# A float64-weight attention and gated feed-forward kernel on one core: conversions begun inside the first attention pass and done in halves, the second queries loaded ahead of the values, and the first value means written in place

## The chip, the cores and the metric

The kernel runs on one NeuronCore of a Trainium2 chip. The metric is device time of one execution in microseconds (us). A core has a matrix engine (PE, with weight loads shown as PEld), a vector engine (DVE), a scalar engine (ACT), a GpSimd engine (POOL) and a queue that issues DMA transfers (SP). Each engine runs its own instructions strictly in their order and waits on semaphores for the others.

## The reference

```python
scores_l = scale * q @ k.T                     # |i - j| < 16 kept, else -1e9
k_sum    = max of k over blocks of 32 keys     # 24 per head
v_sum    = mean of v over blocks of 32 keys
scores_s = scale * q @ k_sum.T + log(32)
a        = softmax(concat(scores_l, scores_s)) # denominator + 1e-9
attn     = a @ concat(v, v_sum)                # (4, 8, 768, 64)
x        = attn as (3072, 512)
out      = (x @ w_a * (x @ w_b)) @ w_out       # d_ff = 1536
```

q, k and v are float32. The three weight matrices are float64 in memory: `w_a` and `w_b` are 512 x 1536, `w_out` is 1536 x 512.

## The kernel before, in words

The 3072 tokens are cut into 12 units of 256 tokens (u = 0 to 11), three to each of four batches. A unit has an attention pass, `attention(u)`, over two tiles of 64+64 queries, and then 12 items (u, f), one for each slice of 128 of the 1536 hidden columns. An item is `hidden(u, f)`: 24 matmuls of 128x256 into one PSUM bank (12 with w_a, 12 with w_b), then `g` on ACT and DVE (L586, L587), then its split into `gh` (ACT, L590) and `gl` (POOL, L591). `down(u, f)` adds its 6 matmuls of 128x512 into `po` (L569).

Each float64 weight is turned on the chip into two float32r tiles, `hi` and `lo`. There are 36 conversions: slices f = 0 to 11 of w_a, w_b and w_out, called a0, b0, o0, a1 and so on. One conversion (`convert_weights`) is one ACT instruction (L159, `p`), four DVE instructions of 128x512 in a chain (L161 into PSUM tile `s`, L164 into `f`, L170 into `s`, L173 into `p`), an ACT copy to `hi` (L181) and two POOL instructions (L182, L183, the second gives `lo`). `raw` and `w` have the same memory, so L181 overwrites what L173 has read. The tiles `f` and `p` come from the pool `stage` (six buffers, tag t2k). A raw load waits for the conversion four before it (`AHEAD = 4`).

The head of the program is written out by hand: `load_first` loads k, q and v of unit 0; `attention(0)` runs to its end; then nine conversions are written; then the items, the first `LAG = 5` of them of unit 0 alone, and after them unit 1 and unit 0 by turns. Each of the first items brings three conversions with it, later ones two. A scheduler then orders each engine's instructions by a time model of its own, so that the program order is a priority rather than an order; the order that comes out is fixed when the kernel is built. The k loads of batch 1 (`blocks`, L293) wait for the last conversion.

In the head, `sum_first_v` makes the 24 block means of v with six matmuls of 24x512, copies them to a tile `vs` (L208), and `load_vsums` (L402) moves `vs` by four DMAs into the rows of the value tiles `vw` that `av` (L480) reads. Two of the six v tiles lie in `pt` and one in `kin` and one in a `stage` buffer; the second tile's scores `s1` and its two value tiles take four more `stage` buffers, so that five of the six buffers are taken by the first attention pass.

Of the kernel before, what the change touches and what calls it, by code (L numbers as in the profile page):

```python
# [21 lines left out]
def attention_moe(  # L22
# [88 lines left out]
    mean = const.tile([P, 2 * NS - 4], F32, name="mean")  # L111
    nc.gpsimd.memset(mean, 0.0)
    for i in range(P // BLK):
        nc.gpsimd.memset(mean[i * BLK : (i + 1) * BLK, NS - 4 + i, None], 1.0 / BLK)
# [27 lines left out]

    def convert_weights():
        for f, nm in ((f, nm) for f in range(NF) for nm in "abo"):
# [3 lines left out]
            low, high = words[:, :, :, 0], words[:, :, :, 1]  # L148
# [5 lines left out]
            fv = fv.rearrange("p (m n) -> p m n", n=n)  # L154
            pv = pv.rearrange("p (m n) -> p m n", n=n)
            sv = ps_a.tile([P, CV], F32, tag="psc", name=f"s_{nm}{f}")
            sv = sv.rearrange("p (m n) -> p m n", n=n)
            fi, pi, si = fv.bitcast(I32), pv.bitcast(I32), sv.bitcast(I32)
            nc.scalar.mul(out=pv, in_=high.bitcast(F32), mul=2.0**-112)  # L159
# [4 lines left out]
            nc.vector.scalar_tensor_tensor(  # L164
                out=fi, in0=pi, scalar=-(1 << 31), in1=si,
                op0=ALU.bitwise_and, op1=ALU.bitwise_or,
# [3 lines left out]
            nc.vector.tensor_scalar(  # L170
                out=si, in0=fi, scalar1=-(1 << 23), scalar2=None, op0=ALU.bitwise_and
            )
            rest = nc.vector.scalar_tensor_tensor(  # L173
                out=pv, in0=low.bitcast(U32), scalar=2.0**-52, in1=sv,
                op0=ALU.mult, op1=ALU.mult,
            )
# [22 lines left out]
    def sum_first_v():  # L199

        ps = psum("vs0", 0)
        for i in range(S // P):
            nc.tensor.matmul(  # L203
                ps[:NS], mean[:, NS - 4 - 4 * i : 2 * NS - 4 - 4 * i], first["v"][i],
                start=(i == 0), stop=(i == S // P - 1),
            )
        vsums[0] = att.tile([NS, H, D], F32, tag="vs", name="vs0", bufs=1)
        nc.scalar.copy(out=vsums[0].rearrange("p h d -> p (h d)"), in_=ps[:NS])  # L208
# [35 lines left out]

    def load_first():

        shape = [P, 2, 512]
        spots = [  # L250
            xp.tile(shape, F32, tag="x0", name="k_in0"),
            xp.tile(shape, F32, tag="x1", name="k_in1"),
            att.tile(shape, F32, tag="qin", name="k_in2", bufs=1),
        ]
        first["k"] = [t[:, i, :] for t in spots for i in range(2)]
        t = xp.tile(shape, F32, tag="x0", name="q_in0")
        first["q"] = t
        t = xp.tile(shape, F32, tag="x1", name="v_in0")
        first["v"] = [t[:, i, :] for i in range(2)]
        first["v"].append(kin[:, :512])  # L260
        first["v"].append(stage.tile([P, 512], F32, tag="t2k", name="v_in3"))
        first["v"] += [pbuf[:, i].rearrange("p c x -> p (c x)") for i in range(2)]
        for nm, i in (
            [("k", i) for i in range(6)] + [("q", 0)] + [("v", i) for i in range(6)] + [("q", 1)]
        ):
            xin = first[nm][:, i, :] if nm == "q" else first[nm][i]
            src = {"k": k, "q": q, "v": v}[nm]
# [4 lines left out]
            yield  # L272

# [105 lines left out]
    def load_v(b, t, spare=False):  # L379

        if spare:
            vw = [stage.tile([P, H, D], F32, tag="t2k", name=f"vw{b}_{t}_{e}") for e in range(2)]
            nc.gpsimd.memset(vw[0][WIN:], 0.0)
            nc.gpsimd.memset(vw[1][32:64], 0.0)
        else:
            vw = vbuf
# [103 lines left out]
    def attention(u):  # L490
# [10 lines left out]
        if u == 0:  # L501
            s1 = [
                stage.tile([P, 512], F32, tag="t2k", name=f"s1_{h}").rearrange(
                    "p (c x) -> p c x", x=P
                )
                for h in range(2)
            ]
        vw = load_v(b, t0)
        qT = prep_q(u, 0, qin)
        yield  # L510
        scores(u, t0, qT, s)
        yield
        qT = prep_q(u, 1, qin)
        yield
        if u == 0:
            scores(u, t1, qT, s1)
            yield
        if r == 0:
            if u == 0:
                sum_first_v()  # L520
            else:
                for hg in range(2):
                    sum_v(b, hg)
                    yield
            load_vsums(b, vw)
        if u == 0:
            vw1 = load_v(b, t1, True)
            load_vsums(b, vw1)
        transp(u, t0, s)
        yield  # L530
        if u:
            scores(u, t1, qT, s1)
# [3 lines left out]
        if u:  # L536
            vw1 = load_v(b, t1)
# [59 lines left out]
    LAG = 5  # L597
# [81 lines left out]
```

## Time and profile before

| | us |
|---|---|
| median of 3 runs | 759.15 (758.52 to 760.43) |
| the profiled execution | 756.2 |
| its span, first to last instruction | 754.3 |

| engine | busy us | share of the span |
|---|---|---|
| PE | 718.0 | 95% |
| PEld | 644.0 | 85% |
| DVE | 410.6 | 54% |
| ACT | 275.9 | 37% |
| POOL | 254.2 | 34% |

A row of a timeline gives the start, the duration (for several merged instructions from the first's start to the last's end), engine, line, operation, output and inputs, shapes, a count, and in brackets the idle time of the engine before it with what ended it. [...] A row of the table by stretches gives the stretch, its length, busy time of PE, PEld, DVE, ACT and POOL with instruction counts, the granted share of the PE clock, the mean busy share of the DMA engines and GB/s moved.

### The profile page before, as it was taken

The numbers are of one execution on the slowest core, as the hardware profiler recorded it, in microseconds if no ns is written. First come the engines' busy times: TensorE is split into PE (matmuls) and PEld (weight loads), VectorE is DVE, ScalarE is ACT, GpSimd is POOL, SyncE is SP. The second block draws the span as 40 slices with busy tenths as digits, with TensorE's granted clock in tenths as the row PEclk, the third lists the DMA queues.
The fourth block names the chain that finished last, engine by engine and source line by source line (L and its number), as shares of the span: only waits on it lengthen the run. The fifth ranks groups of instructions, "written<-read, shape, count | busy, mean of one in ns | idle before, by whom it ended". The sixth has DMA issues, their size and how long they took to land.

```text
span 754.3 us, 15201 instructions
## 1 busy us (share of the span) xinstructions
PE 718.0 (95%) x5964; PEld 644.0 (85%) x5964; DVE 410.6 (54%) x870; ACT 275.9 (37%) x856; POOL 254.2 (34%) x333
## 2 busy tenths in 40 slices
PE   6778899989999999999999999999999999999997
PEld 3467788879899999998999999998999899999996
DVE  3599999965555444366565444367465444344100
ACT  3678765533232322313233422313233423322212
POOL 4467889962122212212122212213122312212111
PEclk9879899999999999999999999999999999999999
DMA  9956546446502103035302103024302101000000
GB/s 220 209 148 181 166 141 185 143 65 114 148 7 50 50 8 64 29 50 101 119 8 50 51 7 65 30 44 90 112 9 50 50 2 44 29 1 21 29 1 29
DMA packets 155888, 55.05 MB, mean 73 GB/s; under 512 B 136376, under 2 KB 148664, under 8 KB 155816
## 3 DMA queue, kind: packets, MB, share of 16 engines
q1 hardware_dynamic: 155816, 54.07, 29.8%
q8 instruction: 47, 0.77, 0.4%
q14 instruction: 25, 0.20, 0.1%
HBM read 47.12 MB, written 6.29 MB: 71 GB/s over the span
## 4 chain that ended last, share of the span: by engine, by line
PE 70%; DVE 14%; POOL 5%; DMA 5%; issue 2%; SPq 2%; ACT 1%; ACTq 0%; DVEq 0%; POOLq 0%
PE h L552 40%; PE po L569 22%; PE s L423 4%; PE av L480 2%; DMA kin<-in_k_dram 2%; SPq L293 1%; DVE pt L472 1%; PE vs L203 1%; DVE s_b L161 1%; POOL f_b L182 1%; POOL w_b L183 1%; DVE kT L325 1%; DVE f_a L164 1%; DVE vp L221 1%; DVE p_a L173 1%
## 5 line engine op out<-in xcount | busy, mean ns | idle before, releaser
L552 PEld LDWEIGHTS h<-x,w_a 128*128 128x128 f32 x1728 | 231.0, 191 | 25.6 <-DVE g L587 8.5
L552 PE MATMUL h<-x,w_a 128*128 128x256 f32 x1728 | 242.1, 283 | 6.8 <-DVE g L587 6.7
L552 PE MATMUL h<-x,w_b 128*128 128x256 f32 x1728 | 225.4, 278 | 2.2 <-POOL w_b L183 2.2
L591 POOL TENSOR_TENSOR gl<-g,gh 128x256 fp32r<-128x256 f32 x144 | 105.8, 737 | 341.8 <-ACT gh L590 324.8
L552 PEld LDWEIGHTS h<-x,w_b 128*128 128x128 f32 x1728 | 211.3, 189 | 4.3 <-POOL w_b L183 2.4
L569 PE MATMUL po<-w_o,gh 128*128 128x512 f32 x576 | 172.4, 404 | 6.2 <-ACT gh L590 6.1
L587 DVE TENSOR_TENSOR g<-h,g 128x256 f32<-128x256 f32 x144 | 59.5, 418 | 192.0 <-ACT g L586 191.4
L586 ACT COPY g<-h 128x256 f32<-128x256 f32 x144 | 52.4, 370 | 227.7 <-PE h L552 225.9
L569 PEld LDWEIGHTS po<-w_o,gh 128*128 128x128 f32 x576 | 98.1, 189 | 25.0 <-ACT gh L590 7.5
L590 ACT CAST gh<-g 128x256 fp32r<-128x256 f32 x144 | 58.0, 406 | 143.5 <-DVE g L587 143.4
L569 PE MATMUL po<-w_o,gl 128*128 128x512 f32 x288 | 100.8, 398 | 0.1
L472 DVE STREAM_TRANSPOSE pt<-s 32x256 f32<-32x256 f32 x216 | 94.3, 436 | 11.4 <-POOL s L452 8.4
L441 ACT ACTIVATE s<-s,nml 128x128 f32<-128x128 f32 x192 | 74.6, 390 | 40.4 <-DVE nml L436 40.4
L452 POOL TENSOR_TENSOR s<-s,nml 128x512 f32<-128x512 f32 x40 | 41.6, 1041 | 98.7 <-DVE nml L447 93.5
L569 PEld LDWEIGHTS po<-w_o,gl 128*128 128x128 f32 x288 | 51.1, 190 | 9.2 <-POOL gl L591 1.0
L430 DVE SCALAR_TENSOR_TENSOR s<-s,mask 128x512 f32<-128x512 f32 x48 | 31.8, 683 | 25.2 <-PE s L423 23.2
L423 PE MATMUL s<-kT,qT 64*64 64x128 f32 x768 | 43.2, 286 | 1.0 <-POOL kT L348 0.8
L423 PEld LDWEIGHTS s<-kT,qT 64*64 64x64 f32 x768 | 31.0, 137 | 9.0 <-issue 1.4
L480 PE MATMUL av<-pt,vw 128*64 128x64 f32 x768 | 31.5, 231 | 5.2 <-DMA vw<-vs 3.8
L446 DVE TENSOR_SCALAR nml<-nml 128x4 f32<-128x4 f32 x48 | 10.7, 223 | 46.9 <-ACT s L441 46.9
L441 ACT ACTIVATION_READ_ACCUMULATOR s<-s,nml 128x1 f32 x192 | 36.0, 187 | 0.0
L480 PEld LDWEIGHTS av<-pt,vw 128*64 128x64 f32 x768 | 26.8, 142 | 10.4 <-ACT s L441 4.0
(81 smaller groups left out, 493.2 us busy)
## 6 DMA issues: line engine op xcount, KB each, us to landing
raw_a<-in_moe_w_a_dram SPq DMA_DIRECT2D x12, 512.0 KB
raw_b<-in_moe_w_b_dram SPq DMA_DIRECT2D x12, 512.0 KB
raw_o<-in_moe_w_out_dram SPq DMA_DIRECT2D x12, 512.0 KB
out_dram<-ob SPq DMA_DIRECT2D x24, 256.0 KB
qin<-in_q_dram SPq DMA_DIRECT2D x144, 32.0 KB
vb<-in_v_dram SPq DMA_DIRECT2D x24, 192.0 KB
kin<-in_k_dram SPq DMA_DIRECT2D x46, 100.0 KB
vw<-in_v_dram SPq DMA_DIRECT2D x20, 192.0 KB
```

The costliest lines, as they stand in the source:

```text
L423: nc.tensor.matmul(banks[h][es, c, :], qT[hs, c, es], kT[hs, c, c0 : c0 + P], start=True, stop=True, tile_position=(h * D, e * QT),)
L430: nc.vector.scalar_tensor_tensor(out=s[h], in0=banks[h], scalar=0.125, in1=mask[:, kind, None, :].broadcast_to([P, NP, P]), op0=ALU.mult, ...
L441: nc.scalar.activation(s[h][:, c, :], s[h][:, c, :], AF.Exp, bias=nml[:, 0, h, c : c + 1], scale=1.0, accum_out=nml[:, 1, h, c : c + 1],)
L452: nc.gpsimd.tensor_tensor(out=s[h], in0=s[h], in1=l[:, :, None].broadcast_to([P, NP, P]), op=ALU.mult)
L472: nc.vector.transpose(out=pv[js, :, qs], in_=sv[qs, :, js])
L480: nc.tensor.matmul(ps[h * D : (h + 1) * D, c, es], vw[e][:, 2 * c + h, :], pbuf[:, h, c, es], start=True, stop=True, tile_position=(0, h * D),
L552: nc.tensor.matmul(ps, wts[nm, f][:, c, part, :], x[xpart][:, c, :], start=(i == 0), stop=(i == n - 1))
L569: nc.tensor.matmul(po[j], g[:, js], w[:, 0, part, :], start=(f == 0 and i == 0), stop=(f == NF - 1 and i == 2),)
L586: nc.scalar.copy(out=g, in_=pa)
L587: nc.vector.tensor_tensor(out=g, in0=pb, in1=g, op=ALU.mult)
L590: nc.scalar.copy(out=gh, in_=g)
L591: nc.gpsimd.tensor_tensor(out=gl, in0=g, in1=gh.bitcast(F32), op=ALU.subtract)
```

## The change

Five edits, all in the first fifth of the program.

1. A conversion's four DVE instructions of 512 columns become eight of 256 columns, two halves by turns, through one PSUM tile `scratch` that all conversions share.
2. Two conversions (a0, b0) are written behind the first scores, one (o0) behind the second scores, and six at the end of `attention(0)`, where nine stood. `LAG` is 4 instead of 5.
3. The second queries are loaded ahead of the weights and of v, and the v loads take pairs of rows (runs of 512 bytes instead of 256).
4. k, q, v, `s1` and the second value tiles of the first pass lie in nine tiles (`spot`) that later hold the weights of f = 11, 10 and 9, so that they take no `stage` buffer, no `kin` and no `pt`.
5. The block means of v are made by twelve matmuls of 128x256 with a wide indicator matrix `mean` (one memset, two small memsets, four selects on POOL), whose output has the 24 means and 8 zero rows already on the rows that `vw` needs. Four ACT copies (L234) write them there. The four DMAs are gone, and so are two memsets.

```diff
-    mean = const.tile([P, 2 * NS - 4], F32, name="mean")
+    mean = const.tile([P, P + 16], F32, name="mean")
...
+    scratch = ps_a.tile([P, CV], F32, tag="psc", name="scratch")
...
+            parts = []
+            for i in range(2):
+                cols = slice(i * CV // 2, (i + 1) * CV // 2)
+                parts.append((fv[:, cols], pv[:, cols], scratch[:, cols], lows[:, cols]))
+            for fx, px, sx, _ in parts:
+                nc.vector.tensor_scalar(
+                    out=sx.bitcast(I32), in0=px.bitcast(I32), scalar1=3, scalar2=None,
+                    op0=ALU.logical_shift_left,
+                )
...
-            nc.vector.tensor_scalar(
-                out=si, in0=pi, scalar1=3, scalar2=None, op0=ALU.logical_shift_left
-            )
...
-        for i in range(S // P):
-            nc.tensor.matmul(
-                ps[:NS], mean[:, NS - 4 - 4 * i : 2 * NS - 4 - 4 * i], first["v"][i],
-                start=(i == 0), stop=(i == S // P - 1),
-            )
-        vsums[0] = att.tile([NS, H, D], F32, tag="vs", name="vs0", bufs=1)
-        nc.scalar.copy(out=vsums[0].rearrange("p h d -> p (h d)"), in_=ps[:NS])
+        for g in range(2):
+            for i in range(3):
+                for j in range(2):
+                    nc.tensor.matmul(
+                        ps[:, g * 256 : (g + 1) * 256], mean[:, 16 - 8 * i : 16 - 8 * i + P],
+                        first["v"][3 * g + i][:, :, j * D : (j + 1) * D],
+                        start=(i == j == 0), stop=(i == 2 and j == 1),
+                    )
+        for vw in vws:
+            for e, r0 in ((0, WIN), (1, 32)):
+                rows = slice(r0, r0 + 32)
+                nc.scalar.copy(out=vw[e][rows].rearrange("p h d -> p (h d)"), in_=ps[rows])
...
-            [("k", i) for i in range(6)] + [("q", 0)] + [("v", i) for i in range(6)] + [("q", 1)]
...
+        for nm, i in [("k", i) for i in range(6)] + [("q", 0), ("q", 1)]:
...
+    def spot(i):
+
+        return wp.tile([P, 2, 512], F32, tag=f"w{'abo'[i % 3]}{NF - 1 - i // 3}", name=f"spot{i}")
...
-    LAG = 5
+    LAG = 4
...
-    take(rest, 7)
+    take(rest, 8)
     take(weights, 2)
-    take(rest, 7)
-    for _ in attention(0):
-        pass
+    take(rest, 6)
+    first_attention = attention(0)
+    take(first_attention, 8)
+    take_weights(2)
+    take(first_attention, 2)
+    take_weights(1)
+    take(first_attention, 100)
+    take_weights(6)
     atts = {u: attention(u) for u in range(1, NU)}
-    take_weights(9)
```

The order on DVE behind the last maximum of k (`ks`), before. `s` and `s1` are the scores of the two tiles of unit 0, `nml` their maxima and sums.

```order
L315 TENSOR_REDUCE ks0_208<-tr_k5_249 128x4x4
L430 SCALAR_TENSOR_TENSOR s_171<-s0_0_0_275,mask_94 128x512
L430 SCALAR_TENSOR_TENSOR s_171<-s0_0_1_278,mask_94 128x512
L436 TENSOR_REDUCE nml0_0_293<-s_171 128x4 x2
...
L430 SCALAR_TENSOR_TENSOR s1_1_264<-s0_1_1_322,mask_94 128x512
L436 TENSOR_REDUCE nml0_1_337<-s1_0_263 128x4
L161 TENSOR_SCALAR s_a0_442<-p_a0_441 128x512
L436 TENSOR_REDUCE nml0_1_337<-s1_1_264 128x4
L164 SCALAR_TENSOR_TENSOR f_a0_440<-p_a0_441,s_a0_442 128x512
```

And in the changed kernel, at the same place (`spot7` is the second tile's scores):

```order
L342 TENSOR_REDUCE ks0_212<-tr_k5_253 128x4x4
L174 TENSOR_SCALAR scratch_186<-p_a0_322 128x256 x2
L179 SCALAR_TENSOR_TENSOR f_a0_321<-p_a0_322,scratch_186 128x256 x2
L186 TENSOR_SCALAR scratch_186<-f_a0_321 128x256 x2
L191 SCALAR_TENSOR_TENSOR p_a0_322<-raw_a0_202,scratch_186 128x256 x2
L174 TENSOR_SCALAR scratch_186<-p_b0_339 128x256
L456 SCALAR_TENSOR_TENSOR s_171<-s0_0_0_282,mask_94 128x512
L174 TENSOR_SCALAR scratch_186<-p_b0_339 128x256
L456 SCALAR_TENSOR_TENSOR s_171<-s0_0_1_285,mask_94 128x512
L462 TENSOR_REDUCE nml0_0_300<-s_171 128x4
L179 SCALAR_TENSOR_TENSOR f_b0_338<-p_b0_339,scratch_186 128x256 x2
```

All of conversion a0 now stands ahead of the first scores on DVE, and b0 is woven into them; before, a0 began behind the second tile's scores.

The order on ACT in the changed kernel from the first exponentials to the first `av` (`vw0`, `vw1` and `spot8` are the value tiles):

```order
L467 ACTIVATE s_171,nml0_0_300<-s_171,nml0_0_300 128x128 x8
L467 ACTIVATE spot7_267,nml0_1_378<-spot7_267,nml0_1_378 128x128 x4
L163 ACTIVATE p_o0_400<-raw_o0_319 128x512
L467 ACTIVATE spot7_267,nml0_1_378<-spot7_267,nml0_1_378 128x128 x4
L201 CAST w_b0_349<-f_b0_338 128x4x128
L163 ACTIVATE p_a1_496<-raw_a1_336 128x512
L234 COPY vw0_173<-vs0_426 32x512
L234 COPY vw1_174<-vs0_426 32x512
L234 COPY spot8_271<-vs0_426 32x512 x2
L488 COPY pt_172<-pt0_0_0_414 128x512
L201 CAST w_o0_410<-f_o0_399 128x512
L488 COPY pt_172<-pt0_0_1_420 128x512
```

Before, L208 and the first copy to `pt` stood behind the first eight exponentials, and the second tile's exponentials behind both. Now all sixteen, three conversion steps and the four copies stand ahead of `pt`.

The order on DVE behind the last conversion (o11), before (`kT` is built from the k of batch 1, `g1_7` is item (1, 7)):

```order
L173 SCALAR_TENSOR_TENSOR p_o11_1478<-raw_o11_1413,s_o11_1479 128x512
L325 STREAM_TRANSPOSE kT_87<-kin_177 128x6x96
L326 STREAM_TRANSPOSE kT_87<-kin_177 128x6x32
L327 STREAM_TRANSPOSE kT_87<-kin_177 128x32
...
L587 TENSOR_TENSOR g0_11_1818<-h0_11_1793,g0_11_1818 128x256
L587 TENSOR_TENSOR g1_7_1856<-h1_7_1831,g1_7_1856 128x256
```

And now:

```order
L191 SCALAR_TENSOR_TENSOR p_o11_1625<-raw_o11_1554,scratch_186 128x256 x2
L608 TENSOR_TENSOR g0_11_1968<-h0_11_1943,g0_11_1968 128x256
L608 TENSOR_TENSOR g1_8_2006<-h1_8_1981,g1_8_2006 128x256
L512 TENSOR_TENSOR x2_1_2017<-av2_4_2221,x2_0_2016 128x4x128
L352 STREAM_TRANSPOSE kT_87<-kin_177 128x6x96
```

The two products `g` stood behind the transposes of `kT` and now stand ahead of them; beside the last item of unit 0 stands item (1, 8) of unit 1, where it was (1, 7).

## Rows read from the trace of the kernel before

**Rows 1.** The page: the span, and busy tenths of PE and DVE in 40 slices of 18.9 us.

```profile
span 754.3 us, 15201 instructions
...
PE   6778899989999999999999999999999999999997
...
DVE  3599999965555444366565444367465444344100
```

**Rows 2.** Busy time by stretches: start and end, length, then PE, PEld, DVE, ACT, POOL with counts, granted PE clock, DMA share, GB/s.

```profile
15.00:42.50 27.50, 21.72 (x193) 13.11 (x190) 16.86 (x33) 15.43 (x48) 10.29 (x10) 0.88 0.96 205
42.50:112.80 70.30, 58.83 (x473) 50.75 (x472) 65.86 (x116) 54.57 (x160) 53.29 (x46) 0.88 0.54 158
112.80:158.00 45.20, 40.60 (x288) 37.13 (x288) 41.78 (x67) 23.65 (x47) 42.73 (x39) 1.00 0.44 137
158.00:170.00 12.00, 10.13 (x62) 9.44 (x61) 5.93 (x18) 2.49 (x6) 5.11 (x6) 0.86 0.63 101
170.00:754.30 584.30, 577.03 (x4899) 526.89 (x4897) 275.99 (x633) 174.03 (x581) 133.52 (x177) 1.00 0.21 47
```

**Rows 3.** The chain that ended last, from the first scores to the first `av`: start, us, what.

```profile
15.17 1.30 DVE s L430 x2
16.52 7.86 PE vs L203 x12
24.40 0.57 ACT vs L208
25.00 6.01 DMA vw<-vs
...
31.14 1.55 PE av L480 x32
```

**Rows 4.** DVE in order of time, 15 to 42.5 us.

```profile
15.17 1.29 DVE L430 SCALAR_TENSOR_TENSOR s<-s,mask 128x512 f32<-128x512 f32 x2 [2.68 <-PE s L423]
...
26.83 1.29 DVE L430 SCALAR_TENSOR_TENSOR s<-s,mask 128x512 f32<-128x512 f32 x2 [6.14 <-PE s L423]
28.04 0.68 DVE L436 TENSOR_REDUCE nml<-s 128x4 f32<-128x512 f32 x1
28.63 0.68 DVE L161 TENSOR_SCALAR s_a<-p_a 128x512 int32<-128x512 int32 x1
29.22 0.68 DVE L436 TENSOR_REDUCE nml<-s 128x4 f32<-128x512 f32 x1
...
39.42 0.68 DVE L486 TENSOR_TENSOR x<-av,x 128x512 fp32r<-128x512 f32 x1
...
41.81 0.68 DVE L173 SCALAR_TENSOR_TENSOR p_o<-raw_o,s_o 128x512 f32<-128x512 uint32 x1
```

**Rows 5.** DVE in order of time where a conversion follows a conversion, 119 to 125 us.

```profile
119.61 0.69 DVE L161 TENSOR_SCALAR s_a<-p_a 128x512 int32<-128x512 int32 x1
120.41 0.69 DVE L164 SCALAR_TENSOR_TENSOR f_a<-p_a,s_a 128x512 int32<-128x512 int32 x1
121.13 0.69 DVE L170 TENSOR_SCALAR s_a<-f_a 128x512 int32<-128x512 int32 x1
121.86 0.69 DVE L173 SCALAR_TENSOR_TENSOR p_a<-raw_a,s_a 128x512 f32<-128x512 uint32 x1
122.65 0.69 DVE L161 TENSOR_SCALAR s_b<-p_b 128x512 int32<-128x512 int32 x1
...
124.81 0.75 DVE L587 TENSOR_TENSOR g<-h,g 128x256 f32<-128x256 f32 x2
```

**Rows 6.** POOL in order of time, one round of three conversions, 123 to 133 us.

```profile
123.33 1.29 POOL L182 TENSOR_TENSOR f_a<-f_a,w_a 128x512 f32<-128x512 f32 x1 [0.34 <-ACT w_a L181]
124.70 1.28 POOL L183 TENSOR_TENSOR w_a<-f_a,p_a 128x512 fp32r<-128x512 f32 x1
125.93 1.44 POOL L591 TENSOR_TENSOR gl<-g,gh 128x256 fp32r<-128x256 f32 x2
...
132.96 1.29 POOL L182 TENSOR_TENSOR f_a<-f_a,w_a 128x512 f32<-128x512 f32 x1 [0.34 <-ACT w_a L181]
```

**Rows 7.** The chain that ended last, two pieces from 170 us on, where PE alone sets the time: the matmuls of one `hidden` and of one `down`.

```profile
174.92 1.37 PE po L569 x6
176.29 2.75 PE h L552 x24
```

**Rows 8.** DVE in order of time behind the last conversion, 157 to 165 us, and PE beside it.

```profile
157.35 0.69 DVE L173 SCALAR_TENSOR_TENSOR p_o<-raw_o,s_o 128x512 f32<-128x512 uint32 x1
162.29 0.78 DVE L325 STREAM_TRANSPOSE kT<-kin 128x576 f32<-128x576 f32 x1 [4.25 <-DMA kin<-in_k_dram]
...
164.31 0.74 DVE L587 TENSOR_TENSOR g<-h,g 128x256 f32<-128x256 f32 x2
...
164.77 2.78 PE L552 MATMUL h<-x,w_a 128*128 128x256 f32 x12 [1.87 <-DVE g L587]
```

**Rows 9.** Two stretches with the rate of the transfers as the last column: 11 to 13 us (rows of 1 KB, weights) and 14 to 20 us (rows of 256 bytes, v).

```profile
11.00:13.00 2.00, 1.20 (x5) 0.72 (x4) 1.05 (x2) 1.23 (x3) 0.36 (x2) 1.00 1.09 349
14.00:20.00 6.00, 4.55 (x26) 1.39 (x21) 2.82 (x6) 2.91 (x15) 0.70 (x1) 1.00 1.34 218
```

**Rows 10.** The page's costliest groups: the exponentials (mean ns of one behind the comma).

```profile
L441 ACT ACTIVATE s<-s,nml 128x128 f32<-128x128 f32 x192 | 74.6, 390 | 40.4 <-DVE nml L436 40.4
```

**Rows 11.** POOL in order of time, the copy of the key maxima into `kT`.

```profile
12.64 1.05 POOL L348 COPY kT<-ks 128x144 f32<-128x144 f32 x4 [2.76 <-DVE ks L315]
```

More of the change, by code (lines that the diff above doesn't have):

```diff
@@ L243, in turned, with pairs @@
         return tr
+    def pairs(x, b, i, heads=slice(0, H)):
+        return x[b, heads, 256 * i : 256 * (i + 1), :].rearrange("h (p t) d -> p h (t d)", t=2)
     def load_first():
[L249 to L253, printed above, removed]
-        ]
[L255 to L263, printed above, removed]
-            [("k", i) for i in range(6)] + [("q", 0)] + [("v", i) for i in range(6)] + [("q", 1)]
-        ):
+        spots = [spot(i) for i in range(7)]
+        first["k"] = [t[:, i, :] for t in spots[:3] for i in range(2)]
+        first["q"] = spots[3]
+        first["v"] = [
+            t[:, i, :].rearrange("p (h x) -> p h x", x=2 * D) for t in spots[4:] for i in range(2)
+        ]
+        for nm, i in [("k", i) for i in range(6)] + [("q", 0), ("q", 1)]:
             xin = first[nm][:, i, :] if nm == "q" else first[nm][i]
-            src = {"k": k, "q": q, "v": v}[nm]
+            src = k if nm == "k" else q
             nc.sync.dma_start(
@@ L272, in load_first @@
             yield
+        for i, t in enumerate(first["v"]):
+            nc.sync.dma_start(
+                out=t, in_=pairs(v, 0, i % 3, slice(i // 3 * 4, i // 3 * 4 + 4))
+            )
+            yield
+    def spot(i):
+        return wp.tile([P, 2, 512], F32, tag=f"w{'abo'[i % 3]}{NF - 1 - i // 3}", name=f"spot{i}")
     first = {}
@@ L381, in load_v @@
         if spare:
-            vw = [stage.tile([P, H, D], F32, tag="t2k", name=f"vw{b}_{t}_{e}") for e in range(2)]
-            nc.gpsimd.memset(vw[0][WIN:], 0.0)
-            nc.gpsimd.memset(vw[1][32:64], 0.0)
+            spare = spot(8)
+            vw = [spare[:, e, :].rearrange("p (h d) -> p h d", d=D) for e in range(2)]
         else:
@@ L501, in attention @@
         if u == 0:
[L502 to L509, printed above, removed]
+            t = spot(7)
+            s1 = [t[:, h, :].rearrange("p (c x) -> p c x", x=P) for h in range(2)]
+        vw = vw1 = load_v(b, t0)
+        if u == 0:
+            vw1 = load_v(b, t1, True)
+        qTs = [prep_q(u, 0, qin)]
         yield
-        scores(u, t0, qT, s)
+        scores(u, t0, qTs[0], s)
         yield
-        qT = prep_q(u, 1, qin)
+        qTs.append(prep_q(u, 1, qin))
         yield
         if u == 0:
-            scores(u, t1, qT, s1)
+            scores(u, t1, qTs[1], s1)
             yield
[L518 to L524, printed above, removed]
+        if r == 0 and u:
+            for hg in range(2):
+                sum_v(b, hg)
+                yield
             load_vsums(b, vw)
-        if u == 0:
-            vw1 = load_v(b, t1, True)
-            load_vsums(b, vw1)
         transp(u, t0, s)
         yield
+        if u == 0:
+            sum_first_v((vw, vw1))
+            yield
         if u:
-            scores(u, t1, qT, s1)
+            scores(u, t1, qTs[1], s1)
             yield
```

50 lines of the change are left out of this document (30 added, 20 removed).

## The prediction, written before the result was known

> **What bounds the kernel now.** I read the slices of the page first, because a share over the whole span hides stages: PE's digit stays at 9 only from the tenth slice (170 us) on, while DVE's is 9 from the third to the eighth (38 to 151 us) [rows 1]. The table by stretches says the same in numbers. [...] So the tail is work of PE that this change leaves alone; what can be won is what PE stands or runs slowly ahead of 170 us. In 42.5 to 158 that is 70.3 - 58.8 + 45.2 - 40.6 = 16.1 us of standing and about 0.12 x 58.8 = 7.1 us of low clock: 23.2 us.
>
> What holds PE there are the 36 conversions. The three done by 42.5 us end at 41.81 + 0.68 [rows 4], the last at 157.35 + 0.69 [rows 8], so 33 follow in 115.5 us, 3.5 us each. Where nothing stands between them a round of three takes 132.96 - 123.33 = 9.63 us [rows 6]; PE needs 2 x (2.75 + 1.37) = 8.24 us for the two items of a round [rows 7].
>
> **The conversions begin earlier (edits 2, 3, 4).** Between 15 and 42.5 us DVE is busy 16.9 of 27.5 us; the longest gap, 6.14 us, ends with the second tile's scores [rows 2, 4]. Now a0 goes ahead of the first scores and b0 and o0 between the scores, and five `stage` buffers are free for them. Weights a0 come after one more q load of 256 KB, 1.2 us at 218 GB/s [rows 9]. In the trace they are among the 1-KB rows moved from 11 us on, done by about 12 and later now by that 1.2, so DVE can begin near 15 us, when the first scores began. Three conversions earlier, at the 2.9 us that one costs DVE in the filled stretch (below), is 8.6 us. Bounds: nothing, if the inputs come late, and 10 us, all the idle time of the stretch. I take 7, since o0's first step stands on ACT between exponentials and its load now follows six v loads and six value loads, so that both may wait for it.
>
> The price: the first scores' evacuation waits for a0, about 2.7 us. The chain to the first `av` ran from the means (16.52 to 24.38) over a copy of 0.57 and DMAs of 6.01 us to 31.14 [rows 3]. The DMAs go; four copies of about 0.57 come, 2.3 us. That alone would give 6.0 - 1.7 = 4.3 us. But ACT now does all sixteen exponentials, 16 x 0.39 = 6.2 us [rows 10], three conversion steps and the copies ahead of `pt`, so I put unit 0's last `x`, at 39.42 + 0.68 before [rows 4], within 2 us of where it was, at 39 to 42, and count nothing. The wide matmuls stream the same 3,072 columns as before: nothing. On POOL two memsets and four small selects come ahead of the copy into `kT`, where POOL stood 2.76 us waiting for DVE [rows 11], and two memsets go: nothing; without that cover, 1 us.
>
> **The halves (edit 1).** In a dense conversion the steps start 0.80, 0.72, 0.73 and 0.79 us apart, 3.04 together, although one takes 0.69: each waits for the one before [rows 5]. Where independent instructions alternate, 512 columns start 0.59 apart (28.04, 28.63, 29.22) and overlap by some 0.09 [rows 4]. Two `g` of 256 columns end 0.75 after the first began [rows 5]; with the tail of one, 0.42, they start 0.33 apart. Eight halves, each depending on the one two before, are then 8 x 0.33 = 2.64: 0.40 less than the dense chain. In the first 19 conversions other instructions already stand between the steps: the 40 others in that stretch, at their spacing (0.6 for 512 columns, 0.33 for `g`, 0.2 for the small ones), are about 15.5 us, which leaves (70.3 - 15.5)/19 = 2.9 us for a conversion, so the halves give about 0.23 there, 4.4 us. In the last 14 POOL is in the way: of its 9.63 us it stands 0.34 [rows 6], so a round cannot fall below 9.29: 14/3 x 0.34 = 1.6 us. Sum 6.0. Bounds: 33 x 0.40 = 13.2 if POOL never held it, and 13 us lost if halves do not overlap at all (second rival).
>
> **LAG 4 and the end of the conversions (edit 2).** One more item of unit 1 is done by the last conversion, so one less, 2.75 + 1.37 = 4.1 us, stands behind it, if PE keeps up. Also DVE no longer meets the `kT` transposes ahead of the two `g`: before, they waited 4.25 us for a k load and PE 1.87 us for `g` [rows 8]. That 1.87 goes; the k load still comes only after the last conversion and holds the next `g`, by when PE has a hidden item of 2.75 us to do.
>
> **The sum.** From the conversions: 7 + 6 + 4.1 = 17.1 us. PE cannot take all of that. Between 112.8 and 158, at full clock, it still stood 4.6 of 45.2 us, a tenth, because each round has it wait for `g` and for DVE's queue. With the same tenth over the some 102 us that would be left, it loses 10 us; 23.2 - 10 = 13.2 is the most this stretch can give back. I take the smaller, 13.2, add 1.9 for the `kT` stall, and take off 1 for the later first scores: 14 us. The span becomes 754.3 - 14 = 740.3, the profiled execution 742.2 with the 1.9 us around the span. The median of the runs before is 759.15, 2.95 above the profiled execution; on that scale the prediction is 745.1, so 745. With 17.1 + 1.9 and no deduction it is 740; with the conversions' terms halved, 752. The likeliest case's own range is 740 to 751.
>
> **Rivals.**
>
> *All of it passes.* PE hardly waits once unit 1's `x` is there early, its clock stays at the upper level from 40 us on, and DVE fills every gap: 10 + 8 + 4.1, capped by PE's 23.2 less 5 and the stall, gives 20 to 22 us: 738. For it: the clock of 0.88 ahead of 112.8 us [rows 2] comes with PE's standing. Against: three engines that are each nine tenths full seldom all run without waiting for each other.
>
> *Halves do not overlap; it gets slower.* If each half waits for the one before it to end, 8 x 0.42 = 3.4 us per conversion; if it also bears the start-up of a dependent step, 0.04 to 0.11 us (0.72 to 0.80 less 0.69) [rows 5], 8 x 0.50 = 4.0, which is 33 x about 1.0 = 33 us more on the engine that bounds, against 7 + 4.1 + 1.9 won: 20 us slower, and 11 by the lower start-up: 770. It decides from a spacing of about 0.42 us on, where 33 x 0.4 us eats the rest. For it: the change puts 132 more instructions on the fullest engine. Against: the 0.59 us spacing, with a wait on DVE's own semaphore between.
>
> [...] The trace disagrees: neighbours that do not depend on each other overlap by 0.09 us [rows 4]; so I leave this case 0.03.
>
> *The attention passes hold it; little comes out.* Unit 0's `x` is not earlier, DVE's queue in order waits at every `g` for a PE that is now behind, and conversions done early only lie ready. Then LAG's item and the stall remain, 4 to 6 us: 754. For it: PE's first item began when `x` was there, and the second unit's pass is on the same engines. Against: a1 and b1 are needed right after, and DVE, not `x`, was full from 42 to 112 us.
>
> *The change does not do what it says*, since the first conversion waits so long for its load that the scores stand behind it in DVE's queue. Each microsecond of delay there is one of `x`; 4 us of it with the other terms leaves 750, inside my range, so it has no chance of its own.
>
> **How the numbers follow.** Forecast 0.60; all passes 0.13; little comes out 0.17; halves without overlap and no change 0.03; slower by the halves 0.07. The range is to leave two in ten: 738 to 756 takes in the forecast, half of the first rival and most of "little". A measurement of this kernel can tell about 0.3%, 2.3 us, from no change. Faster by more takes the forecast, the first rival and 0.13 of "little", 0.86; within 0.3% are 0.03 of "little" and the 0.03, 0.06; slower are 0.07 and the last 0.01 of "little", 0.08.
>
> **What would show it.** Right: a0's four steps near 15 us on DVE as pairs 0.33 us apart; the sixth conversion done by about 43 us where three were; the last near 145; rounds of three near 9.3 with POOL without gaps; PE's clock above 0.88 between 42 and 113; no idle of PE behind `kT`. Wrong: pairs 0.42 apart or more; DVE idle ahead of the first scores for more than 3 us; unit 0's `x` later than 43; or rounds still at 9.6 with PE, not POOL, without gaps.

## The result, and the profile after the change

The changed kernel takes 761.82 us (median of 20 runs, 758.58 to 764.11) against 757.21 us for the kernel before in the same comparison (20 runs). The ratio is 1.0052, with a 95% interval of 1.0038 to 1.0067: half a per cent slower, where 2% faster was forecast and 756 was the end of the range. The profiled execution has a span of 757.6 us at a mean clock of 0.986.

The page of the changed kernel, span and slices of 18.9 us, against [rows 1]:

```profile
span 757.6 us, 15351 instructions
...
PE   7598888789999999999999999999999999999997
...
DVE  4899999885565345267375345268465344344110
```

DVE's digit is 8 in the second slice, where it was 5, and 9 from the third to the seventh; but it is still 8 in the ninth, where it had fallen to 6. The same stretches as in [rows 2] (length, then PE, PEld, DVE, ACT, POOL with counts, clock, DMA share, GB/s):

```profile
15.00:42.50 27.50, 18.80 (x201) 14.71 (x197) 23.85 (x62) 19.41 (x56) 15.40 (x13) 0.81 0.95 235
42.50:112.80 70.30, 60.21 (x536) 52.07 (x535) 65.95 (x171) 50.57 (x155) 46.47 (x42) 1.00 0.49 143
112.80:158.00 45.20, 36.71 (x241) 32.29 (x240) 40.93 (x104) 19.88 (x41) 36.19 (x33) 0.96 0.46 140
158.00:170.00 12.00, 10.26 (x52) 8.94 (x51) 9.47 (x25) 4.21 (x9) 9.95 (x9) 0.72 0.06 9
170.00:757.60 587.60, 577.90 (x4909) 526.96 (x4908) 280.68 (x649) 175.11 (x584) 136.01 (x181) 1.00 0.22 49
```

The start did what was forecast: DVE is busy 23.85 us of the first stretch (16.86 before), and six conversions are over at 46.4 us where the sixth ended at 54.9. Then the lead is lost. DVE is as busy as before in the second stretch, but POOL, which finishes the conversions, is busy 46.5 us instead of 53.3. The remaining 30 conversions take 122 us (103 before), and the last one ends at 168.3 us instead of 158.0.

DVE in order of time, the first conversion and one in a dense stretch, against [rows 5]; x2 is the two halves of one step, and the duration runs from the start of the first to the end of the second:

```profile
15.16 0.89 DVE L174 TENSOR_SCALAR scratch<-p_a 128x256 int32<-128x256 int32 x2 [2.16 <-ACT p_a L163]
...
127.02 0.89 DVE L174 TENSOR_SCALAR scratch<-p_b 128x256 int32<-128x256 int32 x2
128.02 0.75 DVE L179 SCALAR_TENSOR_TENSOR f_b<-p_b,scratch 128x256 int32<-128x256 int32 x2
128.80 0.89 DVE L186 TENSOR_SCALAR scratch<-f_b 128x256 int32<-128x256 int32 x2
129.73 0.75 DVE L191 SCALAR_TENSOR_TENSOR p_b<-raw_b,scratch 128x256 f32<-128x256 uint32 x2
130.59 0.43 DVE L174 TENSOR_SCALAR scratch<-p_o 128x256 int32<-128x256 int32 x1
...
167.51 0.75 DVE L191 SCALAR_TENSOR_TENSOR p_o<-raw_o,scratch 128x256 f32<-128x256 uint32 x2
```

The last row is the end of the last conversion. A half takes 0.42 to 0.43 us. Where a pair takes 0.75, its second half began 0.33 after the first; where it takes 0.89, it began 0.46 after, when the first had ended. From 127.02 to 130.59 a conversion costs 3.57 us; before it was 3.04.

POOL in order of time, against [rows 6]:

```profile
120.13 1.29 POOL L202 TENSOR_TENSOR f_b<-f_b,w_b 128x512 f32<-128x512 f32 x1 [0.83 <-ACT w_b L201]
121.50 1.28 POOL L203 TENSOR_TENSOR w_b<-f_b,p_b 128x512 fp32r<-128x512 f32 x1
...
131.27 1.29 POOL L202 TENSOR_TENSOR f_b<-f_b,w_b 128x512 f32<-128x512 f32 x1 [0.84 <-ACT w_b L201]
```

A round, from `f_b` to `f_b`, takes 11.14 us where it took 9.63, and POOL stands 0.8 to 0.9 us in front of two of the three conversions of a round (b and o) for a cast on ACT, which waits for DVE. Since the last conversion ends 10.2 us later and the span is only 3.3 longer, what stands behind the last conversion is 589.4 us instead of 596.3.

### The profile page after: what moved, and what is told of

Read it like the earlier page. It is cut to its first block, busy times and chain, and to the rows that moved or that the text cites. A ratio compares the mean times of both kernels' runs of the same rounds, so it can differ in the third digit from the quotient of the medians.

```text
span 757.6 us, 15351 instructions
## 1 busy us (share of the span) xinstructions
PE 713.8 (94%) x5976; PEld 641.8 (85%) x5976; DVE 425.0 (56%) x1014; ACT 276.0 (36%) x859; POOL 253.7 (33%) x333
## 4 chain that ended last, share of the span: by engine, by line
PE 70%; POOL 9%; DVE 6%; SPq 5%; issue 5%; DMA 3%; ACT 2%; POOLq 0%; ACTq 0%; DVEq 0%
PE h L573 41%; PE po L590 22%; PE s L449 3%; PE av L506 3%; DMA kin<-in_k_dram 1%; POOL gl L612 1%; POOL f_b L202 1%; POOL w_b L203 1%; SPq L320 1%; SPq L421 1%; POOL w_a L203 1%; DMA vb<-in_v_dram 1%; POOL w_o L203 1%; POOL f_a L202 1%; POOL f_o L202 1%
## 5 line engine op out<-in xcount | busy, mean ns | idle before, releaser
L573 PEld LDWEIGHTS h<-x,w_a 128*128 128x128 f32 x1728 | 227.9, 189 | 19.6 <-issue 2.4
L573 PE MATMUL h<-x,w_a 128*128 128x256 f32 x1728 | 237.7, 281 | 2.1 <-DVE x L512 1.0
L590 PEld LDWEIGHTS po<-w_o,gh 128*128 128x128 f32 x576 | 99.8, 192 | 36.8 <-ACT gh L611 18.4
L590 PE MATMUL po<-w_o,gl 128*128 128x512 f32 x288 | 99.2, 399 | 0.2
L467 ACT ACTIVATE s<-s,nml 128x128 f32<-128x128 f32 x184 | 71.5, 391 | 35.5 <-DVE nml L462 35.5
L478 POOL TENSOR_TENSOR s<-s,nml 128x512 f32<-128x512 f32 x38 | 39.5, 1040 | 82.2 <-DVE nml L473 77.3
```

Of the source, the lines that this page charges most:

```text
L467: nc.scalar.activation(s[h][:, c, :], s[h][:, c, :], AF.Exp, bias=nml[:, 0, h, c : c + 1], scale=1.0, accum_out=nml[:, 1, h, c : c + 1],)
L478: nc.gpsimd.tensor_tensor(out=s[h], in0=s[h], in1=l[:, :, None].broadcast_to([P, NP, P]), op=ALU.mult)
L573: nc.tensor.matmul(ps, wts[nm, f][:, c, part, :], x[xpart][:, c, :], start=(i == 0), stop=(i == n - 1))
L590: nc.tensor.matmul(po[j], g[:, js], w[:, 0, part, :], start=(f == 0 and i == 0), stop=(f == NF - 1 and i == 2),)
```

## The experiments

Theory 1: the two halves use one PSUM tile, and so six of the eight halves wait for the instruction directly ahead of them. The built program says so. Conversion b10, where no other instruction stands between the steps, has these waits; each wait for `DVE_49`, DVE's own semaphore, is for the instruction directly ahead (the number in a semaphore's name plays no part):

```
L174 TENSOR_SCALAR scratch_186<-p_b10_1485 128x256 [waits DVE_49] x2
L179 SCALAR_TENSOR_TENSOR f_b10_1484<-p_b10_1485,scratch_186 128x256 [waits DVE_49,Pool_49]
L179 SCALAR_TENSOR_TENSOR f_b10_1484<-p_b10_1485,scratch_186 128x256
L186 TENSOR_SCALAR scratch_186<-f_b10_1484 128x256 [waits DVE_49] x2
L191 SCALAR_TENSOR_TENSOR p_b10_1485<-raw_b10_1410,scratch_186 128x256 [waits DVE_49,DMAHW3_49]
L191 SCALAR_TENSOR_TENSOR p_b10_1485<-raw_b10_1410,scratch_186 128x256
```

The second halves of L179 and L191 write SBUF and wait for nothing. The second halves of L174 and L186 write `scratch`, and wait for the first half although it writes other columns of it. The rival is that something else in the change costs the time: the early placement, the means in place, or LAG 4.

**Undivided conversions, all else kept** (and, in the other experiments that keep the conversions whole, this edit too):

```diff
-            for i in range(2):
-                cols = slice(i * CV // 2, (i + 1) * CV // 2)
+            for i in range(1):
+                cols = slice(0, CV)
```

> The changed kernel with conversions undivided: four steps of 512 columns, all else of the change kept. Theory 1 (the halves share one PSUM tile, so six of eight wait for the instruction directly ahead, 0.46 us, and only two start 0.33 after it): a dense conversion takes 3.04 us again, rounds 9.6 to 9.8 us, the last conversion is over at 146 to 152 us, and the time is 742 to 748 us, ratio to before 0.980 to 0.988. Rival A (the early placement, the means in place or LAG 4 cost the time): rounds stay above 10.5 us and the time at 755 or more.

Measured: 744.67 us, ratio 0.9843 (0.9822 to 0.9864). A conversion is 3.04 us again, the last one ends at 152.5 us:

```profile
113.46 0.69 DVE L174 TENSOR_SCALAR scratch<-p_a 128x512 int32<-128x512 int32 x1
114.26 0.69 DVE L179 SCALAR_TENSOR_TENSOR f_a<-p_a,scratch 128x512 int32<-128x512 int32 x1
...
116.50 0.69 DVE L174 TENSOR_SCALAR scratch<-p_b 128x512 int32<-128x512 int32 x1
...
151.83 0.69 DVE L191 SCALAR_TENSOR_TENSOR p_o<-raw_o,scratch 128x512 f32<-128x512 uint32 x1
```

**The halves alone, on the kernel before**: its `sv` replaced by `scratch`, and the loops over `parts` of the change.

> The kernel before with the halves alone. Theory 1: 33 conversions of some 0.4 to 0.55 us more each, so the last is over at 171 to 177 us and the time is 12 to 19 us longer, ratio 1.016 to 1.025; the rounds are near 11 us. Rival A: the halves cost nothing by themselves, the time is within 3 us of before and the rounds within 0.2 us of 9.6.

Measured: 769.99 us, 1.018 (1.0155 to 1.0205), the last conversion at 176.9. The two runs agree: the halves cost 13 us on the kernel before and, by the ratios, 16 on the changed one, and all else in the change, taken together, wins 12.6. Rival A is out.

**Halves in two banks**, and its companion with whole conversions. The kernel's pools hold eight PSUM tiles of one bank each (four `po`, two `psh`, `psa` and `psc`), and the second scratch takes `psa` from the attention passes of units 0 and 1:

```diff
-    scratch = ps_a.tile([P, CV], F32, tag="psc", name="scratch")
+    scratch = [ps_a.tile([P, CV], F32, tag=t, name=f"scratch_{t}") for t in ("psc", "psa")]
...
-                parts.append((fv[:, cols], pv[:, cols], scratch[:, cols], lows[:, cols]))
+                parts.append((fv[:, cols], pv[:, cols], scratch[i][:, cols], lows[:, cols]))
...
-        0: cycle([(ps_a, "psa"), (ps_o, "po0"), (ps_h, "psh"), (ps_o, "po1")]),
-        1: cycle([(ps_a, "psa"), (ps_o, "po1")]),
+        0: cycle([(ps_o, "po0"), (ps_h, "psh"), (ps_o, "po1")]),
+        1: cycle([(ps_o, "po1")]),
```

> The changed kernel with the two halves' scratch in two PSUM banks, the second taken from the attention passes of units 0 and 1, so that each half depends on the instruction two before. Theory 1: all eight spacings in a dense conversion are 0.32 to 0.36 us, a conversion 2.6 to 2.8, rounds 9.3 to 9.6 with POOL nearly without gaps, and the time 1 to 5 us below the undivided conversions with the same banks. Rival B (a half has a price of its own, 0.42 us or more whatever it depends on): spacings 0.42 to 0.46, a conversion 3.4 us, rounds near 11, and the time at 755 or more.

> Companion of the two-bank kernel: conversions undivided, one scratch bank, and the attention passes of units 0 and 1 with the same bank fewer. Theory 1: within 3 us of the undivided kernel with all banks, since the passes wait for DVE rather than for a bank; rounds 9.6 to 9.8. Rival C (the passes need the bank): 4 us or more above the undivided kernel, by a later first hidden product.

Measured: 760.84 us (1.0047, 1.003 to 1.0064) with halves, 753.11 us (0.9952, 0.9933 to 0.9972) without. DVE of the two-bank kernel in order of time:

```profile
119.82 0.42 DVE L174 TENSOR_SCALAR scratch_psc<-p_a 128x256 int32<-128x256 int32 x1
120.15 0.42 DVE L174 TENSOR_SCALAR scratch_psa<-p_a 128x256 int32<-128x256 int32 x1
120.47 0.41 DVE L179 SCALAR_TENSOR_TENSOR f_a<-p_a,scratch_psc 128x256 int32<-128x256 int32 x1
120.80 0.41 DVE L179 SCALAR_TENSOR_TENSOR f_a<-p_a,scratch_psa 128x256 int32<-128x256 int32 x1
121.13 0.42 DVE L186 TENSOR_SCALAR scratch_psc<-f_a 128x256 int32<-128x256 int32 x1
...
122.45 0.42 DVE L174 TENSOR_SCALAR scratch_psc<-p_b 128x256 int32<-128x256 int32 x1
...
138.63 0.41 DVE L191 SCALAR_TENSOR_TENSOR p_o<-raw_o,scratch_psa 128x256 f32<-128x256 uint32 x1
```

All starts are 0.32 to 0.34 apart and the conversion takes 2.63 us; the forecast said 2.64. That shows the mechanism: all eight halves now carry a wait on DVE's own semaphore, but for the instruction two before, and the loss per conversion is gone. It also rules out a price of a half by itself (rival B). One thing this run does not separate: two halves that write one bank without a wait between them stand in no version. In the changed kernel the second halves of L179 and L191, which only read the shared bank and wait for nothing, start 0.33 after the first. The last conversion is over at 139.0 us, 29 us earlier than in the changed kernel. So the spacing came out as expected and the time did not: it was to be 1 to 5 us below the companion and is 7.7 above it. The missing bank alone costs 8 us (753.1 against 744.7; rival C's price, but seen in unit 1's second `x`, over at 82.5 us instead of 74.3, and not in a later first hidden product). In the stretch from 165 to 200 us PE is busy 16.9 of 35 us, at a clock of 0.57:

```profile
165.00:200.00 35.00, 16.92 (x147) 13.55 (x146) 22.66 (x54) 9.42 (x31) 1.96 (x6) 0.57 0.68 137
```

Its matmuls show the clock: twelve of `hidden` took 1.56 us ahead of this stretch and 2.76 in it.

```profile
160.45 1.56 PE L573 MATMUL h<-x,w_b 128*128 128x256 f32 x12
...
197.41 2.76 PE L573 MATMUL h<-x,w_b 128*128 128x256 f32 x12
```

PE has done the items of units 0 and 1 by then, and unit 2's attention pass stands open.

**The second part's scratch in SBUF**, so that no bank is taken (264 columns in PSUM, 248 in SBUF):

```diff
+    cut = 264
+    second = const.tile([P, CV - cut], F32, name="second")
...
-                cols = slice(i * CV // 2, (i + 1) * CV // 2)
-                parts.append((fv[:, cols], pv[:, cols], scratch[:, cols], lows[:, cols]))
+                cols = slice(i * cut, (CV - cut) * i + cut)
+                parts.append((fv[:, cols], pv[:, cols], second if i else scratch[:, cols], lows[:, cols]))
```

> The changed kernel with the second part's scratch (248 of the 512 columns) in SBUF, the first part's (264) alone in the PSUM bank, and all banks left to the attention passes: each part depends on the instruction two before. Theory 1: spacings of 0.31 to 0.36 us, a dense conversion 2.5 to 2.8 us, rounds near 9.3 with POOL almost without gaps, the last conversion over by 137 to 146 us; if what is gained there reaches the end, the time is 737 to 742, below the undivided kernel's 744.7 by the 3 to 7 us that the prediction put on the halves. Rival D (the end of the conversions no longer decides; PE runs out of items and the pass of unit 2 stands open): the last conversion as early, PE idle ahead of unit 2's first hidden product, and the time at 744 to 760.

Measured: 777.42 us, 1.0265 (1.022 to 1.0309), the slowest of all. Neither theory had this. DVE and POOL in order of time:

```profile
133.20 0.38 DVE L181 SCALAR_TENSOR_TENSOR f_b<-p_b,second 128x248 int32<-128x248 int32 x1
...
135.14 1.23 DVE L193 SCALAR_TENSOR_TENSOR p_b<-raw_b,second 128x248 f32<-128x248 uint32 x1
...
137.38 1.30 DVE L181 SCALAR_TENSOR_TENSOR f_o<-p_o,second 128x248 int32<-128x248 int32 x1
```

```profile
133.39 1.34 POOL L204 TENSOR_TENSOR f_a<-f_a,w_a 128x512 f32<-128x512 f32 x1 [2.69 <-ACT w_a L203]
134.81 1.29 POOL L205 TENSOR_TENSOR w_a<-f_a,p_a 128x512 fp32r<-128x512 f32 x1
...
137.11 1.30 POOL L204 TENSOR_TENSOR f_b<-f_b,w_b 128x512 f32<-128x512 f32 x1
```

A step with both inputs in SBUF takes 0.38 us when it begins before POOL's instruction, and 1.23 or 1.30 when it begins inside one: it ends about 0.27 after POOL's end (136.37 against 136.10, 138.68 against 138.41). Over the whole trace the 26 such steps that begin outside a POOL instruction take 0.38 to 0.41 us. Of the 46 that begin inside one, 36 take 0.56 to 1.52 and end 0.27 or 0.28 after it; the other ten began within 0.01 us of its start and took 0.41, and there POOL's instruction took 1.54 to 1.58 instead of some 1.3. The second parts of L176 and L188, with one input and the output in SBUF, take longer there too: 0.25 to 0.28 us outside, up to 1.25 inside. The first part, with an input or the output in PSUM, takes 0.39 to 0.44 throughout. So a scratch in PSUM does more than save room here. With 36 of these steps drawn out in this way, the run tells nothing on the halves.

**Where the overlapping halves' gain goes.** Three attempts on the two-bank kernel, all with halves: unit 2's pass begun ten items ahead (`2: item0[2] - 10` in `begin`); unit 2's pass in unit 0's output banks (`2: cycle([(ps_o, "po0")])`), with a companion of whole conversions; and the first of these with unit 3's loads held back.

> The two-bank kernel (760.8 us) with the attention pass of unit 2 spread from ten items ahead of unit 2's first item on, where it was four. Rival D (the two-bank kernel's loss is unit 2's pass, 14.6 us of PE idle at 174 to 195 us and the lower clock behind it): most of that idle goes, and the time is 744 to 752. Against it (the missing bank in the earlier passes costs it): the time stays at 757 or more.

> The two-bank kernel (760.8 us) with unit 2's attention pass in the two banks of unit 0's output, which are free by then, where it had one bank that the scratch held until the last conversion. Rival G (the one shared bank made unit 2's pass late, and so hid what overlapping halves give): the 14.6 us of PE idle at 174 to 195 us shrink to under 5 and the time is 738 to 748. Against it (DVE's queue has unit 3's loads and transposes ahead of unit 2's steps whatever the bank): the time stays above 755.

> Companion of the kernel above: the same banks, but conversions undivided (753.1 us with unit 2's pass in one bank). Expected 745 to 753. The difference to the kernel above is what halves give when they overlap: by the prediction's term 3 to 7 us in favour of the halves, by its bound 13 at most; if unit 2's pass or POOL's work decides, nothing or a loss.

Measured: 758.06 us (1.0013, 0.9992 to 1.0033); 753.73 us (0.9938, 0.9919 to 0.9956); companion 763.24 us (1.0073, 1.0049 to 1.0097). The first met the case against rival D by its time, though the idle of PE is in the same place as before; the second lies between its two cases; the companion came out 10 us above what was expected of it. With the first pair of banks the halves cost 7.7 us against whole conversions, with the second they win 9.5. Unit 2's second `x` moves the same way: 194.8 us against 191.9 in the first pair, 189.4 against 199.4 in the second. So what overlapping halves are worth goes with what happens to unit 2's pass, and no single number was found for it. In the kernel with the early pass, DVE's queue shows one thing that holds it:

```profile
187.75 0.59 ACT L511 CAST x<-av 128x512 fp32r<-128x512 f32 x1 [2.08 <-PE av L506]
190.07 0.78 DVE L352 STREAM_TRANSPOSE kT<-kin 128x576 f32<-128x576 f32 x1 [4.71 <-DMA kin<-in_k_dram]
...
192.09 0.68 DVE L512 TENSOR_TENSOR x<-av,x 128x512 fp32r<-128x512 f32 x1
```

Unit 2's last step, L512, had its input from ACT at 188.34 (ACT's copy starts at 187.75 and takes 0.59), but begins only at 192.09: it stands behind unit 3's key transposes, which wait 4.71 us for their load. In the thirteen profiles up to there the span ends 562 to 566 us after that step. So unit 3's first loads were made to wait for it:

```diff
-                    tc.add_manual_dep(load.ins, converted[-1].ins.name, after, reason="pace")
+                    pace = xdone[5] if b == 1 and row <= 0 else converted[-1]
+                    tc.add_manual_dep(load.ins, pace.ins.name, after, reason="pace")
```

(with the same wait on the loads of `vb`; `xdone` lists the L512 instructions). It was run on the two-bank kernel with the early pass and on the undivided kernel.

> The two-bank kernel with unit 2's pass ten items ahead (758.1 us), and unit 3's first loads of k, q and v made to wait for unit 2's second x instead of the last conversion, so that DVE's queue has none of unit 3's transposes and sums ahead of unit 2's steps. In eleven of the kernels looked at, the span ends 562 to 566 us after unit 2's second x. Theory 3 (what overlapping halves win is lost because unit 2's x waits in DVE's queue behind unit 3's transposes, which wait for their loads): that x is ready at 165 to 175 us where it was at 192.8, and the time is 729 to 742. Against it (the pass is long by its own steps, or PE has its units 0 and 1 to do until then): that x at 185 or later and the time at 750 or more.

> The undivided kernel (744.7 us) with the same wait of unit 3's first loads for unit 2's second x. Theory 3: that x comes at 175 to 179 us where it was at 180.2, since the conversions end at 152 and leave less to win, and the wait of PE behind the transposes, 1.86 us, goes: 739 to 744. Against it: within 1 us of 744.7, or later because unit 3's pass is now late.

Measured: 755.46 us (0.9972, 0.9953 to 0.9992) and 749.8 us (0.991, 0.9878 to 0.9942). Unit 2's last step is now over at 179.9 us, 12.9 earlier than at 192.8, between the two cases put, and yet the time falls by only 2.6. Two stretches, and the second `x` of units 2 and 3 where it is not shown above, first with the early pass and then with the waits as well:

```profile
165.00:200.00 35.00, 18.25 (x144) 15.03 (x145) 22.90 (x55) 8.98 (x30) 2.51 (x7) 0.56 0.62 135
200.00:260.00 60.00, 60.00 (x516) 54.00 (x515) 26.59 (x62) 19.87 (x70) 14.14 (x18) 1.00 0.18 39
...
249.58 0.69 DVE L512 TENSOR_TENSOR x<-av,x 128x512 fp32r<-128x512 f32 x1 [1.33 <-ACT x L511]
```

```profile
165.00:200.00 35.00, 26.66 (x231) 23.85 (x228) 13.08 (x35) 11.09 (x37) 2.81 (x5) 0.85 0.49 94
200.00:260.00 60.00, 53.96 (x470) 47.22 (x469) 39.45 (x87) 19.16 (x73) 14.67 (x21) 0.97 0.37 79
...
179.16 0.69 DVE L514 TENSOR_TENSOR x<-av,x 128x512 fp32r<-128x512 f32 x1 [6.07 <-ACT x L513]
...
246.37 0.69 DVE L514 TENSOR_TENSOR x<-av,x 128x512 fp32r<-128x512 f32 x1 [0.96 <-ACT x L513]
```

PE stands 8 us less before 200 us and 6 us more after it. Unit 3's transposes and sums now fall behind 200 us (DVE is busy 39.5 of those 60 us where it was 26.6), and unit 3's second `x` gains only 3.2 us, 247.1 against 250.3. On the undivided kernel the same wait makes unit 3's second `x` 6 us later (243.5 against 237.4) and costs 5 us. Theory 3 has the queueing right, but the remedy moves the hole, and the 562 to 566 us were no constant: with the waits they are 573 and 575. One unit later there is one. In all fifteen profiles, these two among them, the span ends 505 to 508 us after unit 3's second `x`, and it is this step that a version has to bring forward. That a conversion done earlier can't be had in the end without attention passes done earlier is what these runs support; a version that has both was not found.

**The other terms.** LAG 5 on the undivided kernel; the nine conversions behind the whole first pass; and the same with the second tile's scores and values back in `stage`:

```diff
-            t = spot(7)
-            s1 = [t[:, h, :].rearrange("p (c x) -> p c x", x=P) for h in range(2)]
+            s1 = [
+                stage.tile([P, 512], F32, tag="t2k", name=f"s1_{h}").rearrange(
+                    "p (c x) -> p c x", x=P
+                )
+                for h in range(2)
+            ]
```

> The undivided kernel (744.7 us) with LAG 5. By the prediction's term one more item, 4.1 us, stands behind the last conversion: 747.5 to 750. Rival E (LAG changes nothing, since PE has the same items to do and only their order differs): within 1.5 us of 744.7.

> The undivided kernel (744.7 us) with the first nine conversions behind the whole first attention pass again; the order of loads, the means in place and LAG 4 are kept. By the prediction's term the conversions begin 7 us later, of which the first scores give back 1: 749 to 752. Rival F (an early start only lets conversions lie ready): within 2 us of 744.7.

> The undivided kernel with the nine conversions behind the first pass in the code (744.2 us) and, in addition, the second tile's scores and its values back in four of the six stage buffers. Theory 2 (the conversions begin early because the stage buffers are free, not because of the place in the code): the third conversion ends near 40 us where it ended at 31.8, and the time rises by 5 to 8 us, to 749 to 752. Rival F (an early start only lets conversions lie ready): within 2 us of 744.2.

Measured: 748.79 us (0.9881, 0.9841 to 0.9922), 744.17 us (0.9823, 0.9781 to 0.9865) and 750.51 us (0.9886, 0.9852 to 0.992). LAG 4 is worth 3 to 4 us, though the two intervals overlap. Placing the conversions behind the first pass in the code undid nothing: built, that kernel has the same instructions with the same waits in the same order on every engine as the undivided one. The third conversion's last step starts at 31.08 in it, so that run tests no early start; it is the undivided kernel measured again, 744.2 us against 744.7. It starts late only when the `stage` buffers are taken:

```profile
31.08 0.69 DVE L191 SCALAR_TENSOR_TENSOR p_o<-raw_o,scratch 128x512 f32<-128x512 uint32 x1
```

```profile
39.17 0.68 DVE L191 SCALAR_TENSOR_TENSOR p_o<-raw_o,scratch 128x512 f32<-128x512 uint32 x1
```

With them taken, the last conversion ends at 158.0 us instead of 150.9, and the time rises by 5 to 6 us, with intervals that overlap at their ends. The undivided kernel, in both its measurements, beats the kernel before and the changed one.

## Why the prediction was wrong, point by point

- **The halves: the step that failed.** The prediction put "Eight halves, each depending on the one two before, are then 8 x 0.33 = 2.64". In the changed kernel two of the eight carry no wait, and the other six wait for the instruction directly ahead, which makes 3.57 us of the conversion, 0.53 more than whole steps and not 0.40 less. The term was put at 6 us won; the runs show 13 to 16 us lost. The duration of a half (0.42) and the spacing of independent ones (0.33) were right, and the two-bank run shows 2.63. What was not read was which tile the waits were kept for. The order of the changed kernel with its waits showed it beforehand.
- **The second rival named this outcome.** It asked for 3.4 to 4.0 us per conversion, deciding "from a spacing of about 0.42 us on". The mean spacing was 3.57 / 8 = 0.446 and the loss 13 to 16 us. It had a chance of 0.07, because the prediction set against it the spacing in [rows 4], which was of instructions in different tiles. Its price for the lower start-up is added up wrongly: 8 x 0.46 = 3.68, so 33 x 0.64 less the 13 won is 8 us slower and not 11. With the 3.57 measured the same sum gives 33 x 0.53 - 13 = 4.5 us, where 4.6 was measured. The case of halves without overlap and no change, which had 0.03, leaves the time at 759, the nearest of all to the result, but by luck: no run shows halves that never overlap. The second halves of L179 and L191 here, and all eight in the two-bank run, start about 0.33 us after the one ahead, which takes 0.41 to 0.42.
- **The conversions begin earlier: right.** 7 us were taken; the run with the `stage` buffers taken shows 5 to 6 of the time and 7.1 of the last conversion. The free buffers do it, not the place in the code.
- **LAG 4: right as far as the runs tell**, 3 to 4 us for 4.1, with intervals that overlap.
- **The `kT` stall: right in the changed kernel, and back in the undivided one.** As forecast, the two `g` run ahead of the transposes. PE still waits 0.97 us for them, where [rows 8] had 1.87, but what DVE waits for is ACT's copy and no load. In the undivided kernel the built order has the transposes in front of the two `g` again, and PE waits 1.86. DVE, first the changed kernel, then the undivided one:

```profile
172.25 0.76 DVE L608 TENSOR_TENSOR g<-h,g 128x256 f32<-128x256 f32 x2 [3.98 <-ACT g L607]
...
173.62 0.77 DVE L352 STREAM_TRANSPOSE kT<-kin 128x576 f32<-128x576 f32 x1
```

```profile
156.89 0.78 DVE L352 STREAM_TRANSPOSE kT<-kin 128x576 f32<-128x576 f32 x1 [4.38 <-DMA kin<-in_k_dram]
...
157.95 0.71 DVE L608 TENSOR_TENSOR g<-h,g 128x256 f32<-128x256 f32 x2
```

- **The first scores: right.** Unit 0's second `x` is over at 41.6 us (40.1 before).
- **The sum without the halves: near, and partly by luck.** Undivided, the change wins 12.6 us; the forecast's terms without the halves are 7 + 4.1 + 1.9 - 1 = 12.0. But the 1.9 was not won there, and the two terms measured one by one are 5 to 6 and 3 to 4 us. That leaves some 3 to 5 us to the rest of the change, the loads and the means, which no run separates.
- **"PE cannot take all of that": the cap was too kind.** The prediction took 10 us of loss in the stretch as what limits PE. The 7.1 us of low clock in its 23.2 are an estimate, 58.8 us times what the 0.88 of [rows 2] lacks to 1; no run shows that price by itself. In the changed kernel the clock from 42.5 to 112.8 us was 1.00, and PE was busy 60.2 us with 536 instructions where it had been 58.8 with 473. The two-bank run has the conversions over at 139 us, earlier than the 145 that the prediction put, and PE busy 48.7 of 50 us between 115 and 165, and still no gain, since unit 2's pass is then the open end. So even a right size for the halves' term would have been counted at the wrong place: no version with overlapping halves came below the undivided kernel's 744.7 us, though one of them beat its own companion by 9.5.
- **The signs listed.** Pairs 0.33 apart: only two of four. Sixth conversion by 43: 46.4. Last near 145: 168.3. Rounds near 9.3: 11.1, POOL with gaps. Clock above 0.88 in 42 to 113: yes, 1.00. No idle of PE behind `kT`: none for the transposes, 0.97 us for `g`. The idle time of PE lies elsewhere: up to the last conversion it waits eight times for ACT's `gh`, 12.5 us between 42 and 168:

```profile
PE po L590 <- ACT gh L611: 12.5, 8, 1.8
PE h L573 <- POOL w_b L203: 4.0, 5, 1.2
```

In the undivided kernel the first of these is one wait of 1.3 us up to its last conversion.

## What to carry to other kernels

Before instructions are halved so that they overlap, look in the built program at what each half waits for: halves that write one PSUM tile waited for each other here whatever columns they wrote, and the spacing was 0.46 us instead of 0.33. When the work that bounds a stage gets faster, ask which later pass the slower stage had covered; here it was the passes of units 2 and 3, and conversions that were over 13 us earlier than in the undivided kernel came to nothing. An edit that changes the order in the code changes the order on an engine only if the scheduler follows it; here nine conversions moved in the code gave the same built program.

## What the runs showed of the hardware that was not expected

A DVE step of 248 columns with both inputs in SBUF took 1.23 and 1.30 us in the rows shown when it began inside a POOL instruction, and 0.38 ahead of one; with an input or the output in PSUM, 264 columns took 0.39 to 0.44 in both cases. A wait of DVE on its own preceding instruction cost 0.13 us at 256 columns (0.46 against 0.33), and a wait for the instruction two before cost nothing that shows. While PE stood idle for half of the stretch from 165 to 200 us, in the two-bank kernel and in the one with the early pass, its granted clock was 0.57 and 0.56. In the kernel before and the changed one the clock of nearly every half microsecond from 15 to 200 us is 1.00 or 0.50 (361 and 364 of 370), so the two-bank kernel's 0.57 would be, by an estimate from these two values, 0.50 for some 86% of the stretch. In the two-bank kernel twelve matmuls then took 2.76 us instead of 1.56, so that the stall cost more than its own length.
